# Eight fetches of w_out move to GpSimd's queue, and the first piece of w_in is issued by SyncE alone

## The chip, the core and the metric

The kernel runs on one core of a Trainium2 chip. The metric is the device time of one execution in microseconds (us). The core has a tensor engine (PE, with its weight loads shown apart as PEld), a vector engine (DVE), a scalar engine (ACT), GpSimd (POOL) and SyncE (SP). DMA transfers are issued by an engine's instruction queue (here SP's, ACT's, and after the change POOL's) and carried by 16 DMA engines that all queues share.

## The reference

Two steps follow one another. The first is a gated linear attention, computed as a recurrence over time for 4 batches and 8 heads of 48 features, 768 steps each. The second is a block with one hidden layer over the resulting 3072 tokens of 384 features.

```python
for t in range(S):                                    # S = 768, D = 48
    state = alpha[:, :, t, :, None] * state + einsum('bhd,bhe->bhde', k[:, :, t], v[:, :, t])
    y[:, :, t] = einsum('bhd,bhde->bhe', q[:, :, t], state)
x = y.transpose(0, 2, 1, 3).reshape(3072, 384)
h = x @ w_in                                          # w_in 384 x 2048
out = (h - tanh(h)) @ w_out                           # w_out 2048 x 384
```

The inputs q, k, v and alpha are float32. w_in and w_out arrive in 8-byte words and are rounded to float32 on the chip.

## The kernel before

The 3072 tokens are cut into 12 units of 256 tokens (two chunks of 128). For each unit there is a stage of attention (function `gla`) and a stage of the hidden layer (function `moe`) in eight steps of 256 hidden features. In a step, "first" (line 1082, tile h) multiplies the unit's xT with a slice of w_in, ACT and DVE form h - tanh(h) (lines 1091 to 1109), and "second" (lines 1127 and 1148, tile o) multiplies with a slice of w_out. Units 0 and 1 use w_out plainly; later ones use sums of its blocks.

The weights come in 16 pieces of 768 KB, eight of w_in ("in0" to "in7") and eight of w_out ("out0" to "out7"), in the order in0, in1, in2, in3, out0, in4, out1, in5, out2, in6, out3, in7, out4, out5, out6, out7. `fetch` issues one through `load_weight` (the DMA is line 43) into one of four raw buffers; piece n waits until piece n - 4 has been read. A piece of w_in is eight DMAs of 96 KB, a piece of w_out one DMA of 768 KB. `convert` rounds it: two passes on ACT (lines 86 and 87), then two operations on DVE (lines 89 and 90).

For unit 0, alpha, k and q come in "rough" tiles that PE turns by products with the identity (line 664, tiles turned and sc). alpha is then copied to aT by ACT (even rows) and DVE (odd rows, line 671), and DVE scans it (lines 712 and 731, tiles U and W), multiplies kT and qT (line 680), and masks the scores (line 821) that PE made (line 797). PE's further small products are "back" (line 927), "update" (line 940) and "y" (lines 852 to 862), and ACT writes xT (lines 913 and 922). Unit 1 turns k and q in the same way, and takes alpha through DVE's transposes (line 640). For units from 1 on, a last step "moves" copies parts of xT within the memory by six small DMAs on SP (line 1016); the unit's first h reads what they wrote. v is read by line 585, and alpha, k and q of later units by line 601.

The order on each engine is written out ahead of time by the class `Planner`. Every step has a name, an engine, an assumed duration, a rank and what it waits for. The planner simulates them, engine by engine, starting each engine at the time in `plan.begin`, tries eight rounds of priorities, and keeps the best order. Into the gaps that it expects on PE before unit 0's first y it puts filler products (`spin`, line 1210). So a changed assumption can change the order on every engine, far from the edit.

On SP and ACT the DMAs share eight semaphores in turn, so that each issue waits for the landing of the eighth DMA before it.

Of the kernel before, what the change touches and what calls it, by code (L numbers as in the profile page):

```python
# [38 lines left out]
def load_weight(nc, pool, rows, queues=None, **kw):  # L39

    raw = pool.tile([P, WN], I64 if rows[0][2].dtype != FP32 else FP32, name="raw", **kw)
    for n, (at, js, src) in enumerate(rows):
        (queues[n % len(queues)] if queues else nc.sync).dma_start(out=raw[at].rearrange("p (j n) -> p j n", n=src.shape[-1])[:, js], in_=src)  # L43
    return raw


def weight_parts(w_in, w_out, pad_rows, what, s, by_tile=True):

    if what == "out":
        return [(slice(0, P), slice(0, 2), w_out.rearrange("(j p) n -> p j n", p=P)[:, 2 * s:2 * s + 2, :])]  # L50
    parts = []
    for i in range(len(pad_rows[0])):
        at, f0 = pad_rows[0][i]
        step = pad_rows[1][i][1] - f0
        src = w_in[f0:f0 + len(pad_rows) * step].rearrange("(j p) n -> p j n", p=step)
        src = src[0:at.stop - at.start, :, 2 * s * P:2 * (s + 1) * P]

        few = at.stop - at.start < 32 or not by_tile
        parts += [(0, at, slice(0, len(pad_rows)), src)] if few else [(j - 9, at, slice(j, j + 1), src[:, j:j + 1]) for j in range(len(pad_rows))]
    return [x[1:] for x in sorted(parts, key=lambda x: (x[0], x[1].start))]  # L60
# [261 lines left out]
class Planner:  # L322
# [13 lines left out]
    def add(self, name, engine, us, rank, after, do, lat=0.3):  # L336
        kind = name.rsplit(" ", 1)[0]
        self.tasks.append((name, engine, us, rank, [a for a in after if a], do, lat, self.last.get(kind)))
        self.last[kind] = name
# [85 lines left out]
def fast(tc, q, k, v, alpha, moe_w_in, moe_w_out, out, w_in, w_out, ident, ok, pad_rows):  # L425
    nc = tc.nc
# [12 lines left out]
    V, A, T, GP = nc.vector, nc.scalar, nc.tensor, nc.gpsimd  # L439
# [3 lines left out]
    with ExitStack() as ctx:  # L443
# [91 lines left out]
        plan = Planner()  # L535
        add = plan.add
# [11 lines left out]
        pieces = sorted(((what, s) for s in range(FS) for what in RANK), key=lambda x: (RANK[x[0]] + 2 * x[1], x))  # L548
        raw_of = {}

        def fetch(what, s):
            raw_of[what, s] = load_weight(nc, raw_pool, weight_parts(moe_w_in, moe_w_out, pad_rows, what, s),
                                          queues=[A, nc.sync] if (what, s) == pieces[0] else None, bufs=4)

        def convert(what, s):
            it = []

            def begin():
                dst = w_in[:, :, 2 * s * P:2 * (s + 1) * P] if what == "in" else w_out[:, 2 * s:2 * s + 2, :]
                it.append(round_weight(nc, raw_pool, raw_of.pop((what, s)), dst))  # L560
                next(it[0])
            return begin, lambda: next(it[0], None)

        for n, (what, s) in enumerate(pieces):
            rank = RANK[what] + 2 * s
            held = pieces[n - 4] if n >= 4 else None
            add(f"fetch {what}{s}", "SP", 3.0 if n == 0 else 5.0 if n == 1 else 4.3 if what == "in" else 2.0, rank - 30, [held and f"read {held[0]}{held[1]}"],
                lambda what=what, s=s: fetch(what, s), lat=2.5)
            a, b = convert(what, s)
            older = pieces[n - 2] if n >= 2 else None  # L570
            add(f"read {what}{s}", "ACT", 1.9, rank, [f"fetch {what}{s}", older and f"{older[0]}{older[1]}"], a)
            add(f"{what}{s}", "DVE", 1.6, rank, [f"read {what}{s}"], b)
# [486 lines left out]
        for n in range(len(pieces)):  # L1059
            rank = 2 * FS * 3 + 8 * n  # L1060
# [148 lines left out]
                spun.append(ps_o.tile([P, P], FP32, name="spin", tag="o2"))  # L1209
            T.matmul(spun[0], lhsT=ident, rhs=ident, start=True, stop=True)  # L1210
        plan.filler = "PE", "y 0.0", 0.24, spin
        plan.begin.update(SP=0.8, PE=1.5, ACT=5.4, DVE=4.8)

        for u in range(NU):
            gla(u, rank_gla(u))
# [44 lines left out]
def kernel(  # L1260
# [28 lines left out]
    w_out = consts.tile([P, FT, d_model], FP32, name="w_out")  # L1289
    ok = consts.tile([1, 1], I32, name="ok")  # L1290
    fine = fast(tc, q, k, v, alpha, moe_w_in, moe_w_out, out, w_in, w_out, ident, ok, pad_rows)
    with tc.If(fine < 1):
        general(tc, q, k, v, alpha, moe_w_in, moe_w_out, out, w_in, w_out, ident, pad_rows)
# [30 lines left out]
```

## Time and profile before

| | |
|---|---|
| Median of 3 runs | 580.15 us (579.97 to 580.42) |
| The profiled execution's own time | 580.15 us |
| Its span in the profile | 578.4 us |
| Mean granted PE clock | 0.997 |
| PE busy | 565.1 us (98%) |
| DVE busy | 450.8 us (78%) |
| ACT busy | 322.7 us (56%) |
| POOL busy | 4.8 us (1%) |
| DMA, SP's queue (q1) | 48.49 MB |
| DMA, ACT's queue (q10) | 1.38 MB |

Times in the profile count from the start of the span, in us. In rows of the timeline the first number is the start and the second the duration, "SPq" and "ACTq" are DMA issues, and the bracket gives the idle time before and what ended it. The profile counts two PE records for each product with float32 operands, since it takes two passes: a step's six products of line 1082 stand as x12. A row of issues gives the time on the queue, not that of the transfer.

### The profile page before, as it was taken

To read this page: it belongs to the slowest core of one execution; us is meant where nothing else is said; L and a number is where in the kernel's file an instruction comes from. 1 tells how busy PE (TensorE), PEld (TensorE's weight loads), DVE (VectorE), ACT (ScalarE), POOL (GpSimd) and SP (SyncE) were. 2 spreads that over 40 slices of the span, in tenths; PEclk is the share of its full clock that TensorE was granted. 3 is DMA by queue.
4 is the path that set the end of the run, shared out by engine and by line. 5 is a ranking of instruction groups with operands and counts; after the bars stand their busy time and mean duration, and the time that the engine had idled before them with its cause. 6 is when DMAs were issued, how large, how long until landed. Compare 5 with 4: busy or idle time off the path is not lost.

```text
span 578.4 us, 13800 instructions
## 1 busy us (share of the span) xinstructions
PE 565.1 (98%) x5615; PEld 500.1 (86%) x5615; DVE 450.8 (78%) x886; ACT 322.7 (56%) x559; POOL 4.8 (1%) x22
## 2 busy tenths in 40 slices
PE   8889999999999999999999999999999999999995
PEld 8776777778999998998999899898998999899995
DVE  3999899999997895895895896796798645554643
ACT  1869977648776575686484364374443433333530
POOL 3000000000000000000000000000000000000000
PEclk9999999999999999999999999999999999999998
DMA  9888771265755454472710310210200000000001
GB/s 185 208 229 235 267 171 37 75 137 138 125 119 129 124 115 119 123 159 65 192 53 11 85 53 11 67 57 23 51 14 1 29 7 3 28 8 1 27 1 35
DMA packets 60713, 50.84 MB, mean 88 GB/s; under 512 B 35776, under 2 KB 50400, under 8 KB 60640
## 3 DMA queue, kind: packets, MB, share of 16 engines
q1 hardware_dynamic: 57472, 48.49, 33.3%
q10 hardware_dynamic: 3168, 1.38, 1.1%
q8 instruction: 46, 0.75, 0.6%
q14 instruction: 27, 0.22, 0.1%
HBM read 44.04 MB, written 4.72 MB: 84 GB/s over the span
## 4 chain that ended last, share of the span: by engine, by line
PE 92%; DMA 4%; DVE 2%; ACT 1%; issue 1%; SPq 0%; ACTq 0%; DVEq 0%
PE h L1082 42%; PE o L1148 32%; PE o L1127 7%; PE sc L807 2%; PE sc L880 2%; DMA raw<-in_moe_w_in_dram 2%; DMA rough<-in_k_dram 2%; PE sc L890 2%; PE sc L813 2%; PE sc L993 1%; DVE U L712 1%; PE spin L1210 0%; SPq L43 0%; DVE w_in L90 0%; PE y L880 0%
## 5 line engine op out<-in xcount | busy, mean ns | idle before, releaser
L1082 PE MATMUL h<-xT,w_in 128*128 128x256 f32 x1152 | 265.2, 380 | 2.9 <-DVE w_in L90 2.9
L1082 PEld LDWEIGHTS h<-xT,w_in 128*128 128x128 f32 x1152 | 215.6, 190 | 31.7 <-DVE w_in L90 3.7
L1091 ACT ACTIVATE u<-h 128x512 f32<-128x512 f32 x96 | 57.1, 594 | 187.5 <-PE h L1082 187.0
L1099 DVE TENSOR_TENSOR w<-h,u 128x512 f32<-128x512 f32 x96 | 66.0, 688 | 82.0 <-ACT u L1091 81.7
L1148 PE MATMUL o<-b,e 128*128 128x192 f32 x480 | 90.9, 326 | 0.0
L1148 PE MATMUL o<-w_out,e 128*128 128x192 f32 x320 | 81.5, 337 | 0.0
L1148 PEld LDWEIGHTS o<-b,e 128*128 128x128 f32 x480 | 80.2, 190 | 0.0
L1103 DVE SCALAR_TENSOR_TENSOR g<-z,w 128x512 f32<-128x512 f32 x96 | 65.6, 683 | 2.7
L1148 PE MATMUL o<-b,g 128*128 128x192 f32 x320 | 65.1, 326 | 0.0
L1095 ACT ACTIVATE z<-u 128x512 f32<-128x512 f32 x96 | 60.4, 630 | 2.7
L1148 PEld LDWEIGHTS o<-w_out,e 128*128 128x128 f32 x320 | 55.7, 189 | 4.4
L1148 PEld LDWEIGHTS o<-b,g 128*128 128x128 f32 x320 | 54.2, 190 | 0.0
L1109 ACT ACTIVATE big<-u 128x1024 f32<-128x1024 f32 x48 | 50.4, 1050 | 0.0
L1127 PE MATMUL o<-w_out,g 128*128 128x384 f32 x128 | 44.3, 490 | 0.0
L1127 PEld LDWEIGHTS o<-w_out,g 128*128 128x128 f32 x128 | 23.8, 190 | 13.5
L1115 DVE TENSOR_TENSOR e<-g 128x256 f32<-128x256 f32 x80 | 33.7, 422 | 1.8
L1116 DVE TENSOR_TENSOR e<-g 128x256 f32<-128x256 f32 x80 | 33.5, 418 | 0.0
L640 DVE STREAM_TRANSPOSE aT<-ar 128x256 f32<-128x256 f32 x44 | 28.4, 646 | 1.1
L731 DVE TENSOR_TENSOR_SCAN W<-aT,before 128x1032 f32<-128x1032 f32 (+1 forms) x13 | 27.8, 2135 | 0.1
L712 DVE TENSOR_TENSOR_SCAN U<-aT,after 128x1032 f32<-128x1032 f32 (+1 forms) x13 | 27.6, 2132 | 0.1
L1117 DVE TENSOR_TENSOR e<-g 128x128 f32<-128x128 f32 x80 | 22.9, 286 | 0.0
L640 DVE STREAM_TRANSPOSE qT<-qr 128x256 f32<-128x256 f32 x40 | 20.6, 636 | 0.0
(138 smaller groups left out, 559.7 us busy)
## 6 DMA issues: line engine op xcount, KB each, us to landing
raw<-in_moe_w_out_dram SPq DMA_DIRECT2D x16, 768.0 KB, 5.2
raw<-in_moe_w_in_dram SPq DMA_DIRECT2D x76, 96.0 KB, 3.9
raw<-in_moe_w_in_dram SPq DMA_DIRECT2D x16, 288.0 KB, 4.8
vt<-in_v_dram SPq DMA_DIRECT2D x23, 192.0 KB, 3.8
ar<-in_alpha_dram SPq DMA_DIRECT2D x44, 96.0 KB, 2.6
kr<-in_k_dram SPq DMA_DIRECT2D x40, 96.0 KB, 2.4
qr<-in_q_dram SPq DMA_DIRECT2D x40, 96.0 KB, 2.2
out_dram<-cross SPq DMA_DIRECT2D x19, 96.0 KB, 1.7
```

The lines of the kernel that those rows point to most:

```text
L640: V.transpose(to, raws[what][:, g, :, 0:32])
L712: V.tensor_tensor_scan(out=m["U"][:, ns].rearrange("p n t -> p (n t)")[:, ::-1], data0=aT[:, z:a:-1], data1=after[:, a:z][:, ::-1], initia ...
L1082: T.matmul(h[:, a, :], lhsT=w_in[:, j, f * P:(f + 1) * P], rhs=xT[u][:, j, :], start=(j == 0), stop=(j == KT - 1))
L1091: A.activation(m["u", s], m["h", s], AF.Square, scale=W_SCALE ** -1.5)
L1095: A.activation(m["z", s], m["u", s], AF.Square, bias=QB, scale=QA * W_SCALE)
L1099: V.tensor_mul(m["w", s], m["h", s], m["u", s])
L1103: V.scalar_tensor_tensor(out=g.rearrange("p a c t -> p (a c t)"), in0=m["z", s], scalar=QK, in1=m["w", s], op0=ALU.add, op1=ALU.mult)
L1109: A.activation(big, m["us", s // 2].rearrange("p s t -> p (s t)"), AF.Relu, bias=-U_FAST, scale=W_SCALE, accum_out=over[:, n:n + 1])
L1115: V.tensor_add(e[:, 0:2, :], g[:, 0], g[:, 1])
L1116: V.tensor_sub(e[:, 2:4, :], g[:, :, 1, :], g[:, :, 0, :])
L1127: T.matmul(m["o"][c], lhsT=g[:, a, c, :], rhs=w_out[:, f, :], start=(f == 0), stop=(f == FT - 1))
L1148: T.matmul(o[n][:, i], lhsT=g_, rhs=w_, start=(s_ == 0 and (n, i) in ((0, 0), (1, 0), (2, 1), (3, 0))), stop=(s_ == FS - 1), skip_group_ch ...
```

## The change

Three places are edited. w_out's pieces are issued from GpSimd's queue and w_in's from SyncE's, all eight DMAs of in0 among them; before, in0's DMAs alternated between ACT and SP, and all other pieces went through SP. The planner is told so (engine POOL for w_out, 5.7 us of issue for the first two pieces), and its begin times change: ACT 3.0 in place of 5.4, and POOL 6.0, which is new. The tiles and arithmetic stay as they are. In the orders that the planner then writes, PE has 42 filler products in place of 35, and many steps of the first three units stand elsewhere. The first unit's first scores use the banks that alpha's turns left, in both kernels; no line of the diff touches them.

```diff
         def fetch(what, s):
             raw_of[what, s] = load_weight(nc, raw_pool, weight_parts(moe_w_in, moe_w_out, pad_rows, what, s),
-                                          queues=[A, nc.sync] if (what, s) == pieces[0] else None, bufs=4)
+                                          queues=[GP if what == "out" else nc.sync], bufs=4)
...
-            add(f"fetch {what}{s}", "SP", 3.0 if n == 0 else 5.0 if n == 1 else 4.3 if what == "in" else 2.0, rank - 30, [held and f"read {held[0]}{held[1]}"],
+            add(f"fetch {what}{s}", "POOL" if what == "out" else "SP", 5.7 if n < 2 else 4.3 if what == "in" else 2.0, rank - 30, [held and f"read {held[0]}{held[1]}"],
                 lambda what=what, s=s: fetch(what, s), lat=2.5)
...
-        plan.begin.update(SP=0.8, PE=1.5, ACT=5.4, DVE=4.8)
+        plan.begin.update(SP=0.8, POOL=6.0, PE=1.5, ACT=3.0, DVE=4.8)
```

The orders on the engines that the prediction speaks of, in the first 80 us:

| Queue | Before | After |
|---|---|---|
| PE, fillers | 18, 6 and 11 | 18, 3, 6, 6, 6 and 3 |
| PE, first h | behind all turns of unit 1, three conversions of w_in ahead of it | ahead of unit 1's turns, two conversions ahead of it |
| PE, unit 1's first h | behind six o | behind five o |
| SP, between in7 and unit 1's moves | out4 to out7 | v of units 2 and 3 |
| SP, unit 2's alpha, k, q | behind unit 1's moves | among w_in's pieces, ahead of the moves |
| POOL, after its 18 starting operations | nothing until the end | out0 to out7, one behind the other |

## The prediction

> **What bounds the kernel now.** I read the page first: one engine carries the span, and its clock is full.
>
> ```profile
> PE 565.1 (98%) x5615; PEld 500.1 (86%) x5615; DVE 450.8 (78%) x886; ACT 322.7 (56%) x559; POOL 4.8 (1%) x22
> PE   8889999999999999999999999999999999999995
> PEclk9999999999999999999999999999999999999998
> DMA  9888771265755454472710310210200000000001
> ```
>
> PE is at 9 in every slice but the first three (14.5 us each) and the last, so its products can't be hurried; what moves the end is only where PE idles or spins, in the first 50 us. DMA is as full there. The busy time by stretches (sum for PE, PEld, DVE, ACT, POOL; then clock, DMA share, GB/s) says what limits that part:
>
> ```profile
> 20.00:28.00 8.00, 8.00 (x137) 6.56 (x135) 7.54 (x17) 7.29 (x13) 0.00 (x0) 1.00 0.90 221
> 28.00:36.00 8.00, 6.29 (x79) 5.51 (x75) 7.76 (x13) 3.95 (x7) 0.00 (x0) 1.00 0.73 194
> 44.00:52.00 8.00, 6.79 (x144) 4.94 (x143) 7.56 (x14) 6.62 (x11) 0.00 (x0) 1.00 0.80 230
> 60.00:68.00 8.00, 8.00 (x32) 5.87 (x31) 6.33 (x12) 7.01 (x11) 0.00 (x0) 1.00 0.99 381
> ```
>
> DVE is busy 7.5 of each 8 us from 20 to 52, and PE waits for it: the first stage runs on DVE's chain. From 60 to 68 the DMA engines are full. The timeline shows where DVE's chain begins, and what PE waits for (in brackets: idle before, and who ended it):
>
> ```profile
> 6.16 5.60 ACTq L43 DMA_DIRECT2D raw<-in_moe_w_in_dram  x4
> 11.87 0.64 ACT L671 COPY aT<-turned 128x512 f32<-128x512 f32 x1 [6.84 <-DMA raw<-in_moe_w_in_dram]
> 12.54 0.69 DVE L671 COPY aT<-turned 128x512 f32<-128x512 f32 x1 [7.77 <-ACT aT L671]
> 33.98 5.02 PE L1082 MATMUL h<-xT,w_in 128*128 128x256 f32 x22 [1.71 <-DVE w_in L90]
> 47.85 2.43 PE L1082 MATMUL h<-xT,w_in 128*128 128x256 f32 x10 [1.21 <-DVE w_in L90]
> ...
> 57.86 5.83 SPq L43 DMA_DIRECT2D raw<-in_moe_w_out_dram  x4
> 63.74 3.74 SPq L1016 DMA_DIRECT2D xT<-xT  x6
> 75.51 2.98 SPq L585 DMA_DIRECT2D vt<-in_v_dram  x4
> 76.87 2.75 PE L1082 MATMUL h<-xT,w_in 128*128 128x256 f32 x12
> ```
>
> ACT sits 5.60 us on four issues of w_in's first piece, each of which waits for the landing of the eighth DMA before it (the last for v, landed at 10.95), and the copy of alpha queues behind them. The last four rows matter later: the moves of unit 1's xT (63.74) are issued behind w_out's last four pieces, land by 71.4 in the trace, and unit 1's first h (the ninth, 76.87) needs them: 5.5 us of slack.
>
> **Part 1, ACT's four issues leave.** alpha's two turns are the first 32 of 64 products (3.47 us) from 7.47, so done by 9.2. ACT can copy at about 8.4 and DVE at 9.3 instead of 12.54: 3.2 us earlier. SP now issues all eight DMAs of in0; the last still waits for v's landing, so it leaves at 11.4 as now (11.33), and in1's eight follow at 0.465 each until 15.6, as now (15.62). That costs nothing.
>
> **Part 2, the planner's order.** The new begin times (ACT 3.0 for 5.4) make another order. Filler products grow from 35 to 42; after the turns from 17 to 24, at 0.24 us (11 took 2.63). Those 5.8 us are laid between small steps that DVE waits for: PE from 12.8 on has 24 fillers (5.8), two backs (0.8), one update (0.5) and two scores (2.0), so the second scores end near 21.1; DVE's second masks start then instead of 23.07. Of 3.2 us, 2.0 is left; the 1.2 is the fillers' price. The products after it last 3.75 us by their rows, xT is copied at 25.5 (now 28.41), and the first h starts at 26.0 (now 31.56), because it is now placed ahead of unit 1's turns and with two conversions of w_in before it, not three. From there I lay the rows' durations in the new order: turns and h1 until 33.9 (h1 waits for the third conversion, 31.7), back at 36.1 behind DVE's scan of 2.30 and kT's products, h2 until 39.65, scores 40.5, h3 42.2 to 44.8 behind the fifth conversion, the first o until 47.4. The same work (four h, one o, unit 1's first scores) ends at 47.85 + 2.43 = 50.3 now. Gain: **2.9 us** at this point, between 2.0 (only the masks' lead) and 3.7 (all of PE's 5.1 us of idle of 2.2, 1.7 and 1.2 gone, less 1.4 of added fillers).
>
> **Part 3, w_out on POOL.** POOL does nothing after 5.6 us, so nothing is queued behind the eight fetches but the last flag's load, and they wait there for a free raw buffer without holding SP. On SP they took about 0.4 us of issue each plus the waits (5.83 for the last four). No row shows a DMA from POOL. Its nearest rows: on SP one such piece took 0.92 to issue and 4.5 from there to landing, and 2.1 us of transfer (landings at 64.0, 66.1, 68.0, 70.4). The issue could be 0 or several us dearer; ACT waited 1.0 us once for w_out, so pieces have about 1 to 3 us of slack. I take SP's price, and so nothing on the path; 3 us more per piece is a rival.
>
> **Part 4, what SP does with the room.** The new order of SP puts unit 2's alpha, k and q (12 DMAs) and the v of units 2 and 3 (4 DMAs, 192 KB in rows of 192 B) ahead of unit 1's six moves; now they come behind. The 12 lie among w_in's pieces, where DMA has 0.2 to 0.27 of its time free. The v do not: they stand right before the moves, in the stretch where DMA's share is 0.99. One v took 1.1 us alone on SP's queue (landings 36.71 and 37.84), four 4.4. And the fifth and sixth move wait for the first two v to land. So the moves land at 71.4 + 4.4 = **75.8**, if w_out's pieces, now on another queue, are served no later than now. Bounds: 66.5, if queues share evenly by time (SP's last w_in at 60.8, then v, moves), up to 79 if pieces get slower beside each other. I take the upper middle by one sign in the trace's packets: between 8.6 and 8.9 us ACT's queue passed 29 packets of 192 B while SP's passed 30 of 2 KB, so queues alternate by packet and small rows lose against large ones.
>
> When does PE want them? In the new order the ninth h stands one o (2.58) earlier: 76.87 - 2.58 - 2.9 = 71.4. It waits 75.8 - 71.4 = **4.4 us**, with everything on PE behind it. Later nothing waits: the next h, e and stores have PE at 9 in tenths throughout.
>
> **Sum.** Profiled execution 580.15 us, of it span 578.4; the median of the three runs is 580.15 too. 580.15 - 2.9 + 4.4 = 581.65; I say 581.6.
>
> [...]
>
> **Rivals.** (A) *No stall*: the v are read beside w_out without harm, the moves land before 71.4, and 2.9 stays: 577.3 (576.5 to 578.2). For it: two queues at once passed small rows faster at the start (two v in 1.9 us) and the fetches no longer block SP. Against: DMA share 0.99.
> (B) *Slow pieces from POOL*, slower than before: each piece lands 3 us later than from SP. Place: ACT's reads of pieces three to eight (line 86), then DVE's conversion, then o. It decides from about 2 us more per piece, beyond which every o waits for its own; with the stall it gives 581.6 + 2.5 = 584.1 (583 to 586).
> (C) *Nothing changes*: DVE's chain was full anyway, the fillers eat the early start, and the stall is as long as what is left of the gain: 580.1 (579.2 to 581.1). The change then doesn't do what it says for the early stage.
>
> **How the numbers follow.** Forecast 0.46 (579.8 to 583: the gain's 2.0 to 3.7 against a stall of 3 to 5.5), A 0.24, B 0.16, C 0.14. A difference under 0.2% (1.16 us) is about what a measurement of this kernel can't tell from none, so slower begins at 581.3 and faster ends at 579.0. Slower: 0.27 of the forecast and B, 0.43. Same: 0.17 of the forecast and 0.12 of C, 0.29. Faster: A, 0.02 of the forecast, 0.02 of C, 0.28. The range 577.3 to 584.3 leaves out half of A and part of B; cases of both signs hold much of the chance, so the likeliest one's own range, 579.8 to 583.0, stands beside it.
>
> **What would show it.** Right: DVE's copy of aT near 9.3; first h near 26; PE's first o ending near 47.4; then a gap on PE of 3 to 5 us near 71, ended by a DMA of xT, whose moves land near 75; issues of v on SP just ahead of the moves. A: no such gap, PE at 9 throughout, the ninth h near 71.5. B: POOL's pieces take 7 us or more from issue to landing, and line 86 waits for w_out again and again. C: the first o ends near 50. I would be wrong altogether if the end moved after 100 us, where I see no change, or if PE's clock fell below its 9.

## The result and the profile after

The changed kernel takes **590.06 us** (median of 4 runs, 588.2 to 591.39) against 580.28 for the kernel before: 1.0165 times, 95% interval 1.0136 to 1.0195. The prediction was 581.6 us, range 577.3 to 584.3. Its sign was the likeliest one, its size was wrong. The profiled execution took 588.2 us, its span is 586.5; it is the fastest of the four, so the profile below accounts for a loss of some 8 us, and for the 1.9 us between it and the median there is no trace. Of the 52 executions of the kernel before that stand beside the experiments, the 24 with a mean granted clock of 0.994 or 0.995 took 581.4 to 583.3 us and 23 of the other 28 took 579.7 to 580.8, so its medians below differ.

First the page of the changed kernel, the same rows as before the change:

```profile
PE 571.3 (97%) x5629; PEld 504.6 (86%) x5629; DVE 451.3 (77%) x886; ACT 321.8 (55%) x559; POOL 10.9 (2%) x30
...
PE   8999789999999999999999999999999999999995
PEclk9999889999999999999999999999999999999999
DMA  8799951135674555464421120131010000000001
```

The first slices of PE are better than before (8999 for 8889), but the fifth and sixth (59 to 88 us) are a new hole, and in the same two slices the granted clock is below 9. Everything after 88 us is as it was. So the loss lies where the prediction put its one stall; the timeline (PE and DVE) says that it is another one:

```profile
9.33 0.69 DVE L671 COPY aT<-turned 128x512 f32<-128x512 f32 x1 [4.55 <-PE turned L664]
...
64.86 4.32 PE L1082 MATMUL h<-xT,w_in 128*128 128x256 f32 x12 [2.19 <-DVE w_in L90]
...
75.23 4.44 PE L1082 MATMUL h<-xT,w_in 128*128 128x256 f32 x12 [3.24 <-DVE w_in L90]
...
82.19 2.75 PE L1082 MATMUL h<-xT,w_in 128*128 128x256 f32 x12
```

Two h wait for the conversion of w_in, 2.19 and 3.24 us, and each then runs 4.3 to 4.4 us where an h of twelve records took 2.75 before. The forecast wait for xT at the ninth h isn't there: that h starts at 82.19, right behind an o. SP's timeline shows why w_in is late. First the row of in7 before the change, then the changed kernel:

```profile
52.67 5.08 SPq L43 DMA_DIRECT2D raw<-in_moe_w_in_dram  x8
```

```profile
42.50 1.77 SPq L601 DMA_DIRECT2D ar<-in_alpha_dram  x4
44.37 4.53 SPq L43 DMA_DIRECT2D raw<-in_moe_w_in_dram  x8
48.95 3.60 SPq L601 DMA_DIRECT2D kr<-in_k_dram  x4
53.08 5.72 SPq L43 DMA_DIRECT2D raw<-in_moe_w_in_dram  x8
59.13 2.70 SPq L601 DMA_DIRECT2D qr<-in_q_dram  x4
61.94 4.40 SPq L43 DMA_DIRECT2D raw<-in_moe_w_in_dram  x8
66.44 7.51 SPq L585 DMA_DIRECT2D vt<-in_v_dram  x4
74.06 4.10 SPq L1016 DMA_DIRECT2D xT<-xT  x6
```

The three rows of eight are in5, in6 and in7. Unit 2's alpha, k and q stand between them, so in7 leaves SP from 61.94 to 66.34, where it left from 52.67 to 57.75 before; by the trace it has landed at 71.9, before at 60.8. Last the windows (busy time of PE, PEld, DVE, ACT, POOL, then clock, DMA share, GB/s), first two of before, then the changed kernel's:

```profile
60.00:70.00 10.00, 10.00 (x40) 7.41 (x39) 8.17 (x15) 9.01 (x14) 0.00 (x0) 1.00 0.86 325
70.00:80.00 10.00, 10.00 (x40) 7.41 (x39) 8.89 (x11) 8.33 (x14) 0.00 (x0) 1.00 0.77 177
```

```profile
60.00:70.00 10.00, 7.81 (x24) 5.27 (x23) 5.62 (x12) 5.94 (x10) 1.45 (x2) 0.83 1.01 282
70.00:80.00 10.00, 6.76 (x21) 4.68 (x20) 6.11 (x10) 7.79 (x10) 0.72 (x1) 0.83 1.06 242
...
66.00:68.00 2.00, 2.00 (x6) 1.62 (x6) 1.94 (x6) 1.65 (x4) 0.66 (x1) 0.52 0.93 291
68.00:70.00 2.00, 2.00 (x6) 1.35 (x6) 0.87 (x2) 0.00 (x0) 0.00 (x0) 0.62 1.06 306
```

The DMA engines are full in both stretches (before 0.86 and 0.77). The clock isn't a little low: it is half (0.50) for 3.41 us twice, from 66.10 and from 76.34, that is 1.2 and 1.1 us behind the end of each gap. An h at half clock cost 1.57 and 1.69 us more, the o beside them 0.42 together. So the new waits (5.4) and the half clocks (3.7) make 9.1 us, and the early gain (1.4, below) comes off: 7.7. The last product of line 1099 starts at 571.1, before at 563.2: 7.9 us.

### The profile page after: what moved, and what is told of

Its sections match the earlier page's. It is cut to its first block, busy times and chain, and to the rows that moved or that the text cites. A ratio compares the mean times of both kernels' runs of the same rounds, so it can differ in the third digit from the quotient of the medians.

```text
span 586.5 us, 13850 instructions
## 1 busy us (share of the span) xinstructions
PE 571.3 (97%) x5629; PEld 504.6 (86%) x5629; DVE 451.3 (77%) x886; ACT 321.8 (55%) x559; POOL 10.9 (2%) x30
## 4 chain that ended last, share of the span: by engine, by line
PE 86%; DMA 8%; SPq 3%; issue 1%; DVE 1%; ACT 0%; ACTq 0%; DVEq 0%
PE h L1082 40%; PE o L1148 32%; PE o L1127 5%; DMA raw<-in_moe_w_in_dram 4%; PE sc L807 2%; PE sc L880 2%; SPq L43 2%; PE sc L890 2%; DMA rough<-in_q_dram 2%; PE sc L813 1%; DMA vt<-in_v_dram 1%; PE sc L993 1%; DMA qr<-in_q_dram 1%; SPq L601 0%; ACTq L596 0%
## 5 line engine op out<-in xcount | busy, mean ns | idle before, releaser
L1082 PE MATMUL h<-xT,w_in 128*128 128x256 f32 x1152 | 268.5, 384 | 5.7 <-DVE w_in L90 5.7
L1099 DVE TENSOR_TENSOR w<-h,u 128x512 f32<-128x512 f32 x96 | 65.9, 686 | 82.8 <-ACT u L1091 82.5
L86 ACT ACTIVATE more<-raw 128x768 int16<-128x768 uint32 x16 | 17.1, 1070 | 9.3 <-DMA raw<-in_moe_w_in_dram 8.1
(139 smaller groups left out, 573.4 us busy)
```

The lines of the kernel that those rows point to most:

```text
L1082: T.matmul(h[:, a, :], lhsT=w_in[:, j, f * P:(f + 1) * P], rhs=xT[u][:, j, :], start=(j == 0), stop=(j == KT - 1))
L1099: V.tensor_mul(m["w", s], m["h", s], m["u", s])
```

## The experiments

Twelve kernels were run, four at a time beside the kernel before. The theories changed on the way: theory 1, the order on SP; theory 2, GpSimd's queue; theory 3, after e5 and e6, that the queue and the DMA engines have no room at all in that stretch, and each group put ahead makes another late. The edits are given by the changed part of a line alone, or in words behind `#` where the written order is rearranged. In the table "last 1099" is the start of the last product of line 1099 in the profiled execution (563.2 in before); it leaves out the end of the kernel, which differs by up to 2 us between executions. The start differs too: the first fillers take some 420 to 580 ns each, later ones 275, the change comes 4.5 to 7.8 us into the span, and so alpha's turns start at 7.16 us in one profile (e5) and at 8.73 in another (e7), at 7.24 in the changed kernel and at 7.47 in before. So two profiles can be up to 1.6 us apart before any edit matters.

| Run | What it is | Median us (range) | Before, beside it | Ratio (95%) | Last 1099 |
|---|---|---|---|---|---|
| e1 | before, w_out from POOL | 583.6 (582.2 to 587.2) | 580.41 | 1.0058 (1.0032 to 1.0084) | 563.9 |
| e2 | after, w_out from SP | 586.89 (586.2 to 587.3) | 580.41 | 1.0106 (1.0079 to 1.0132) | 570.0 |
| e3 | after, planned with the loads of units 2 and 3 held | 580.35 (579.9 to 581.0) | 580.41 | 0.9986 (0.9972 to 1.0001) | 564.0 |
| e4 | before, in0 on SP, planned for it | 578.51 (577.9 to 580.0) | 580.41 | 0.9967 (0.9952 to 0.9981) | 563.1 |
| e5 | after, k and q of unit 2 behind in7 | 590.66 (590.1 to 590.8) | 581.43 | 1.0171 (1.0154 to 1.0188) | 573.4 |
| e6 | after, v behind the moves | 591.3 (589.9 to 592.6) | 581.43 | 1.0177 (1.0160 to 1.0194) | 575.9 |
| e7 | before, in0 on SP, nothing else | 579.16 (577.7 to 580.6) | 581.43 | 0.9960 (0.9941 to 0.9979) | 562.5 |
| e8 | e4 less eight fillers | **576.84** (576.6 to 577.0) | 581.43 | 0.9935 (0.9918 to 0.9951) | 560.1 |
| e9 | after, k, q and v behind the moves | 581.58 (580.0 to 582.6) | 581.49 | 1.0003 (0.9988 to 1.0018) | 564.3 |
| e10 | e9, w_out from SP | 586.89 (585.7 to 588.8) | 581.49 | 1.0096 (1.0068 to 1.0124) | 568.9 |
| e11 | e8, w_out from POOL | 578.87 (578.4 to 580.0) | 581.49 | 0.9946 (0.9928 to 0.9964) | 562.0 |
| e12 | e8, unit 2's loads early | 584.23 (582.4 to 586.5) | 581.49 | 1.0045 (1.0028 to 1.0063) | 567.2 |

### e1: before, w_out from GpSimd's queue

```diff
-queues=[A, nc.sync] if (what, s) == pieces[0] else None
+queues=[A, nc.sync] if (what, s) == pieces[0] else [GP] if what == "out" else None
```

> The kernel before with its order kept, and only the queue of w_out's eight pieces changed to GpSimd's. Theory 1 (the loss is the order on SP: unit 2's alpha, k and q, 12 DMAs, got ahead of the last pieces of w_in) expects no late w_in: no wait of h for w_in's conversion over 1 us after 55 us, and 579 to 581 us, perhaps a little under the 580.3 of before, since SP has 8 issues of 0.92 us fewer ahead of in7. Theory 2 (the loss is GpSimd's queue itself: its 768 KB transfers take the DMA engines from w_in's 96 KB ones) expects in6 and in7 late here too, waits of h for w_in of 4 us or more in 55 to 80 us, and 585 to 590 us.

Between the two: 3.2 us slower by the median, though PE's waits for w_in are those of before (1.7 and 1.2 us) and the last 1099 is only 0.7 us late; 2.2 us more lie behind the last store in this one profile. There is no late w_in that PE would feel at 55 to 80 us. So the queue alone doesn't make 590, and theory 1 is not refuted, but the queue isn't free either.

### e2: after, w_out from SP

```diff
-queues=[GP if what == "out" else nc.sync]
+queues=[nc.sync]
```

> The changed kernel with its order kept, but w_out's eight pieces issued by SP at their places in that order. Theory 1 (order) expects the late w_in to stay: SP carries 8 issues of 0.92 us more, at least four of them ahead of in7, so in7 is issued at 62 us or later, h waits 5 us or more for w_in in 60 to 80 us, and the time is 588 to 594 us. Theory 2 (GpSimd's queue) expects the waits to go, and 577 to 581 us.

586.89, between the two again: 6.5 us slower than before without GpSimd's queue. The planned order alone costs most of the loss. The waits are spread otherwise: h waits 2.1 us in all for w_in and o 2.1 us for w_out, the longest 1.2 us, and the clock stays at 1.00.

### e3: after, planned with the loads held

```diff
-[u == 1 and ("kUba 0" if what == 3 else "turn qTb 0")]
+[u == 1 and ("kUba 0" if what == 3 else "turn qTb 0"), u in (2, 3) and "moves 1"]
```

> The changed kernel, w_out still from GpSimd, with the loads of alpha, k, q and v of units 2 and 3 held in the plan until unit 1's moves. Theory 1 (order) expects SP to issue in6 by 52 us and in7 by 58 us, no wait of h for w_in over 1 us after 55 us, a granted clock of 1.00 in 60 to 80 us, and 577.5 to 580 us: what is left is the gain of the early part, some 1.6 us by the trace of after (o's first product ends at 48.7 us where the same work ended at 50.3). Theory 2 (GpSimd's queue) expects in6 and in7 late as in the changed kernel, and 586 to 590 us. If the moves behind v were what cost, they are ahead of v here: then the ninth h comes 4 us earlier, but the waits for w_in stay, some 586 us.

580.35, just above what theory 1 expected, and 9.7 us below the changed kernel, with w_out still on GpSimd. No h waits over 0.6 us, the clock is 1.00. The planner moved other steps too (44 fillers), so this is not a clean proof; e5, e6 and e9 move single groups.

### e4 and e7: the first piece of w_in on SP alone

e7 changes only the queue of in0; e4 also tells the planner (5.7 us for in0 and in1, ACT from 3.0 us).

```diff
-queues=[A, nc.sync] if (what, s) == pieces[0] else None
+queues=[nc.sync]
```

> The kernel before with the first piece of w_in on SP's queue alone, the plan told so (5.7 us for in0, ACT free from 3.0 us): the early part of the change without GpSimd's queue. Both theories expect DVE's copy of alpha at 9.3 us where it was 12.5, unit 2's loads behind unit 1's moves as before, no late w_in, and 577.5 to 580 us; 580.3 or more would say that the early part brings nothing, or that its longer line of SP issues makes w_in late by itself.

> The kernel before with one thing changed: the four DMAs of in0 that ScalarE issued are issued by SP. Order and fillers stay as they were. DVE's copy of alpha is expected at 9.3 us (12.5 before), the 2.2 us for which PE waited for kT at 14.5 us gone or halved, and 578 to 580 us. 580.3 or more would say that the earlier copy is lost again before the first h.

Both as expected: 578.51 and 579.16, ratios 0.9967 and 0.9960. This part of the change is good by itself. In e7's profile alpha's turns began late (8.73, the latest of all, so the copy came at 10.82, not 9.3), yet PE's gap of 2.2 us for kT is gone.

### e5: k and q of unit 2 behind in7

```diff
+# in the order that the planner wrote: "load kT 2" and "load qT 2"
+# are taken out and put right behind "fetch in7"
```

> The changed kernel with one thing moved: SP's eight issues for k and q of unit 2, which stand ahead of in6 and in7, come right behind in7; all else keeps its place, w_out stays on GpSimd, v of units 2 and 3 still stands ahead of unit 1's moves. Theory 1 (these loads make w_in late) expects in6 issued by 54 us and in7 by 60 us, h's waits of 2.2 and 3.2 us for w_in at 64 and 75 us under 1.2 us, no half clock there, and 581 to 583 us: some 7 to 9 us less than the changed kernel's 590. If GpSimd's queue alone made w_in late, the waits stay, and 587 us or more. If v ahead of the moves is the loss, as the prediction had it, the waits for w_in go but a wait for xT of some 4 us comes: 584 to 587 us.

A miss: 590.66, no gain. The waits for w_in did fall as theory 1 said (0.9, 1.1 and 0.8 us, in7 landed at 67.6 for 71.9), but the third case of the expectation came, larger than its 4 us. The timeline of e5:

```profile
62.07 1.83 SPq L601 DMA_DIRECT2D kr<-in_k_dram  x4
65.53 2.40 SPq L601 DMA_DIRECT2D qr<-in_q_dram  x4
68.04 10.45 SPq L585 DMA_DIRECT2D vt<-in_v_dram  x4
78.59 3.96 SPq L1016 DMA_DIRECT2D xT<-xT  x6
...
82.62 4.69 PE L1082 MATMUL h<-xT,w_in 128*128 128x256 f32 x12 [6.27 <-DVE U L712]
```

This is the ninth h. The profile names DVE's scan, of which h reads nothing; the fourth of the six moves landed at 82.5. So a stall for xT, as the prediction's Part 4 had it, can happen: 6.27 us, and a half clock with it (mean 0.98 from 70 to 80 us, 0.68 from 80 to 90). But it isn't the stall of v alone. k and q stand ahead of the moves here too, and SP was at them from 62.07 to 67.93; an estimate that takes these 5.9 us off puts the fourth landing at 76.6, where PE had just come free (76.35). No run has v alone in that place. In the changed kernel nothing waits for the moves, since PE is already later than they are.

### e6: only v behind the moves

```diff
+# "load v" of units 2 and 3 also waits for "moves 1"; the rest of the order stays
```

> The changed kernel with only v of units 2 and 3 moved behind unit 1's moves on SP. Theory 1 expects no gain: h still waits 2.2 and 3.2 us for w_in and the clock halves twice, 587 to 591 us. The prediction's own step (v ahead of the moves makes xT late and costs 4.4 us) expects 584 to 586 us.

591.3, at the upper end of what theory 1 expected and not what the prediction's step would have, but with waits of 1.5 and 8.4 us for w_in in place of 2.2 and 3.2:

```profile
61.89 5.28 SPq L43 DMA_DIRECT2D raw<-in_moe_w_in_dram  x8
67.28 4.81 SPq L1016 DMA_DIRECT2D xT<-xT  x6
...
78.63 5.49 PE L1082 MATMUL h<-xT,w_in 128*128 128x256 f32 x12 [8.37 <-DVE w_in L90]
```

in7's last 96 KB were issued at 66.7 and landed at 75.3, while two pieces of w_out of 768 KB (issued by GpSimd at 64.1 and 65.9) landed at 71.1 and 75.2. k and q moved to between in7 and the moves (e5), or v alone moved behind the moves (e6), gain nothing: theory 3.

### e9 and e10: k, q and v behind the moves

```diff
+# "load kT 2", "load qT 2", "load v 2" and "load v 3" are put right behind "moves 1"
-queues=[GP if what == "out" else nc.sync]     # e10 alone
+queues=[nc.sync]
```

> The changed kernel with both moved: k and q of unit 2 and v of units 2 and 3, 12 issues, come behind unit 1's moves on SP; unit 2's alpha stays ahead of in5, w_out stays on GpSimd. Theory 3 (after e5 and e6: SP's line and the DMA engines have no room between 50 and 80 us, so whatever is put ahead makes in7 or the moves late; moving one group only hands the wait to the other) expects no wait of h over 1.5 us, no half clock between 60 and 85 us, and 580 to 583 us. If GpSimd's queue by itself makes in7 late, h still waits 2 us or more for w_in and the time is 585 us or more.

e9 is as expected: 581.58, 8.5 us below the changed kernel with 12 DMAs moved and nothing else; PE, DVE and ACT have the changed kernel's order. Against e6, where v is behind the moves as well and k and q alone stand ahead of in6 and in7, it is 9.7 us less (the two have the same order on PE, DVE and ACT up to some 100 us). in7 landed at 66.7 in e9, still 5.9 us later than before, and that much nobody waits for. PE's waits for w_in in e9, in all and the longest:

```profile
PE h L1082 <- DVE w_in L90: 0.9, 3, 0.4
```

> As e9, but w_out's eight pieces issued by SP at their places in the order. If GpSimd's queue costs 1 to 3 us, as e1 and e2 against the changed kernel say, 578 to 580.5 us; if the queue is free in this order, the same as e9 within 0.7 us.

A miss: 586.89, with a half clock (mean 0.83 from 80 to 90 us). In this order the moved group stands ahead of out6 and out7 on SP:

```profile
71.04 2.86 SPq L585 DMA_DIRECT2D vt<-in_v_dram  x4
73.94 1.42 SPq L43 DMA_DIRECT2D raw<-in_moe_w_out_dram  x2
...
79.85 1.06 ACT L86 ACTIVATE more<-raw 128x768 int16<-128x768 uint32 x1 [10.29 <-DMA raw<-in_moe_w_out_dram]
...
83.03 4.54 PE L1082 MATMUL h<-xT,w_in 128*128 128x256 f32 x12 [4.78 <-DVE w L1099]
```

ACT sits 10.29 us on w_out's piece, its squares of h queue behind, and PE waits for a free bank of h. The edit had made a new late transfer; it says nothing on the queue's price, but shows theory 3 once more with a third victim. Here GpSimd's own queue helped (e9), since its pieces don't stand behind SP's.

### e8: fewer fillers

```diff
-plan.filler = "PE", "y 0.0", 0.24, spin
+plan.filler = "PE", "scores 0.1", 0.24, spin
```

> The kernel of e4 with the last eight fillers (those ahead of the first y) left out, 38 instead of 46. If fillers behind the turns are time of a full PE, y starts some 1.5 to 2 us earlier and the time is 576.5 to 577.5 us, where e4 had 578.5; if PE only waits in their place, for the masks or for w_in, 578 to 579 us; if the wait halves the clock, 579 us or more.

576.84, the best of all: fillers on a full PE are time. The groups of e4 and then of e8 (records, busy us and mean ns, idle before):

```profile
L1210 PE MATMUL spin<-ident 128*128 128x128 f32 x92 | 13.2, 303 | 1.6 <-POOL ident masks.py:199 1.6
```

```profile
L1210 PE MATMUL spin<-ident 128*128 128x128 f32 x76 | 12.3, 328 | 1.6 <-POOL ident masks.py:199 1.6
```

Eight fillers of 0.24 us are 1.9 us; the medians differ by 1.7. PE waits only 0.2 us in e8 between its first product and 130 us.

### e11 and e12: one suspect each, added to e8

```diff
+queues=[GP if what == "out" else nc.sync]                      # e11
+# e12: "load kT 2" ahead of "fetch in6", "load qT 2" ahead of
+# "fetch in7", "load v 2" and "load v 3" ahead of "moves 1"
```

> The kernel of e8 (in0 on SP, 38 fillers, 576.8 us) with w_out's pieces issued by GpSimd, all else the same. A queue that overtakes w_in (e1's 0.7 us in its profile, 3.2 us in its times) expects 577.5 to 580 us; a queue that costs nothing where unit 2's loads stand behind the moves expects 576.3 to 577.3 us.

> The kernel of e8 with unit 2's loads put where the changed kernel has them: k ahead of in6, q ahead of in7, v of units 2 and 3 ahead of unit 1's moves; w_out stays on SP. Theory 3 (the loads put ahead are the main loss) expects h to wait for w_in or for xT some 4 us or more in all between 60 and 85 us, with or without a half clock, and 581 to 585 us. If the loss needs GpSimd's queue, 576.5 to 578.5 us.

Both times are as theory 3 and the queue's price said: 578.87 (2.0 us more than e8, the ranges apart) and 584.23 (7.4 us more). e12's waits are not where theory 3 put them. Where e11's 2 us come from is seen in w_in's DMAs issued from 44 to 60 us. First e8, then e11:

```profile
DMA to landing us min/median/max: 2.9/4.0/5.2
```

```profile
DMA to landing us min/median/max: 3.4/5.6/6.9
```

w_in's 96 KB land 1.6 us later by the median when w_out comes by a queue of its own; in7 has landed at 64.4 for 60.9, and h waits 1.0 and 0.5 us. In e12 no queue is added, and SP's line alone brings the waits (e12's waits of PE from 55 to 110 us):

```profile
PE sc L993 <- DVE kT L736: 2.4, 1, 2.4
PE h L1082 <- DVE w_in L90: 1.6, 1, 1.6
PE h L1082 <- DVE w L1099: 0.7, 2, 0.5
```

h's own waits between 60 and 85 us are 2.3 us, not the 4 expected. The largest ends at 94.68 and is DVE's chain, held up earlier: it waited 3.6 us for out6 at 77.75, which with out7 was issued at 72.9 and 73.6 (in e8 at 65.4 and 66.1), and unit 2's transposes stood behind. Behind the gap an h of twelve records takes 4.00 us in place of 2.75, as at half clock. So part of e12's 7.4 us falls on out6, which in the changed kernel doesn't stand on SP.

So the way from e8 to the changed kernel, in medians: 576.8, 2.0 for GpSimd's queue (e11), 2.7 for the rest of the changed order (e9 against e11), 8.5 for k, q and v put ahead (after against e9): 590.06. The 2.7 is a remainder: that order also has unit 2's alpha ahead of in5 and four fillers more, and no run parted these. The medians of before beside the three groups of runs differ by 1.1 us (580.4 to 581.5), so each step has some 1 us of doubt.

## Why the prediction was wrong

Slower was forecast and slower came, but by another wait than the one in the sum: for the sign that is luck.

**Part 1: right.** DVE copied alpha at 9.33 us, predicted 9.3. SP's part in it cost nothing that shows: in0 and in1 left by 16.5 (15.94 before), and e7 is faster.

**Part 2: right in kind, too large.** The first o ended at 48.8, predicted 47.4, where the same work ended at 50.3: 1.4 us of the 2.9. Two terms were small: the second scores ended at 21.5 for 21.1, and from there to the first h it was 6.0 us (27.56), not 4.9. The list that makes 21.1 adds up to 21.9 as it stands; it comes out if the last three fillers are left behind the scores, as the order has them. And the fillers' price, put at 1.4 us for seven where 0.24 us each makes 1.7, was 2.1 (12.3 us of spins for 10.2).

**Part 3: the price of a piece was right, the place of its cost was not.** From GpSimd a piece took 0.72 us to issue (1.06 the first), and 6.2 us to landing by the median, against 6.6 from SP in the same stretch before. No queue-bound slowness of w_out: rival B's sign failed. But the sum let w_in stand as it was, and w_in's DMAs went from 3.4 to 4.3 us to landing there. That, at 2 us (e11), is what the queue costs. With DVE busy 8.8 of the 10 us from 50 to 60, the two issues there took 0.72 us each. The 2.5 us that rival B's time adds to the sum no run shows: by the medians a piece landed 0.4 us sooner from GpSimd than from SP.

**Part 4: the failed step.** It said of unit 2's alpha, k and q: "The 12 lie among w_in's pieces, where DMA has 0.2 to 0.27 of its time free", and so put them at nothing. Eight of them stand ahead of in6 or in7, and in7 landed 11 us later; some 5 of the 11 are gone in e9, without k, q and v (66.7). The range 0.2 to 0.27 was read from two stretches; the one between them, not shown there, was full:

```profile
36.00:44.00 8.00, 8.00 (x100) 6.79 (x99) 7.56 (x12) 7.53 (x13) 0.00 (x0) 1.00 1.01 262
```

And free shares before the change weren't free after it: w_out's pieces no longer waited their turn behind w_in on SP and came into the same stretch, and DMA's share went to 1.01 and 1.06. k and q alone, put at nothing, cost 9.7 us with v out of the way (e6 against e9); k, q and v together cost 8.5 (the changed kernel against e9), and 7.4 without GpSimd's queue (e12 against e8). So the prices don't add up: k and q alone cost as much as k, q and v. The part's own stall, 4.4 us for v ahead of the moves, didn't come: the moves landed at 81.2, predicted 75.8, and h wanted them at 82.19. Alone it stays untested.

**The bounds.** With a gain of 2.0 to 3.7 and a stall of 3 to 5.5 the forecast's own range is 579.5 to 583.7, a little wider than the 579.8 to 583 given; it would not have held 590 either.

**The sum had no term for the clock.** A clock below its 9 was named as a sign of being wrong altogether, and it fell: 3.7 us of the loss.

The rivals: A (no stall) and C (nothing changes) fell with the first wait; B had the right direction by the wrong victim.

## What to carry to other kernels

When a change moves transfers forward on a queue, sum the issue time and the DMA time of everything that then stands ahead of the transfer that somebody waits for; an average free share of the DMA engines is no room (0.2 to 0.27 in two stretches here, none in the one between them), least of all when the same change sends other bytes by a second queue. Here a queue's order was also a priority: w_out's pieces, taken off SP, no longer waited their turn behind w_in, and w_in's urgent 96 KB landed 1.6 us later (e11). And on a full engine a filler is work: keep fillers only where the engine would wait anyhow (eight fewer gave 1.7 us), but mind the gaps: behind 2.19 and 3.24 us the changed kernel had 3.41 us at half clock each time.

## What the runs showed of the hardware

**Half clock after some gaps.** In the changed kernel gaps of PE of 2.19 and 3.24 us were each followed by 3.41 us at a granted clock of 0.50. In e10 the gap was 4.78 us (mean clock 0.83 from 80 to 90 us), in e12 2.38 us (the h behind it took 4.00 us, not 2.75). Gaps of 1.7 us and less never had it: before (1.71 us) and e12 (1.61 us) show a clock of 1.00 there. Yet before, with 2.19 us at 14.5, and e1, with 2.3 us at 14.7, kept 1.00 too. So the length of a gap alone doesn't tell; what else decides, no run was made to show. After a longer gap it lasted longer: in e6, with 8.37 us, the mean clock was 0.71 from 70 to 80 and 0.78 from 80 to 90, which makes an estimated 10.2 us at half clock.

**Transfers beside a second queue land later.** With w_out on GpSimd's queue and nothing else changed, w_in's 96 KB went from 4.0 to 5.6 us to landing by the median (e8 and e11), and in e6 the last 96 KB of in7 took 8.6 us beside two pieces of 768 KB. How the DMA engines divide themselves between two queues, no run was made to show; the one count of packets is the prediction's (29 beside 30 in 0.3 us of before).
